# Queries kept times 1/128, maxima taken negated, and pooled scores of the last two half batches made one group at a time

## The chip, the cores and the metric

The kernel runs on 1 core of one Trainium2 chip. The metric is device time in microseconds (us), lower is better. One program computes everything in one launch: TensorE (PE) multiplies, VectorE (DVE), ScalarE (ACT) and GpSimd (POOL) work on the results, SyncE (SP) issues the DMAs.

## The reference

Two stages follow each other, all in float32. The first is attention on q, k, v of 2 batches, 8 heads, 576 positions and 64 columns, in two forms that are added:

```python
q_d = q.reshape(B, H, S // 4, 4, D).mean(axis=3)      # the same for k and v: 144 pooled positions
out_d = softmax(scale * q_d @ k_d.T) @ v_d             # scale = 1/8
out_up = np.repeat(out_d, 4, axis=2)
mask = np.abs(pos[:, None] - pos[None, :]) < 4         # each position sees 7 neighbours
out_local = softmax(where(mask, scale * q @ k.T, -1e9)) @ v
attn_out = out_up + out_local
```

The second takes the 1152 x 512 result as tokens x and adds four experts: `out += p[:, e:e+1] * (relu(x @ w1[e]) @ w2[e])`, with w1 of 512 x 1024, w2 of 1024 x 512 and p the normalised domain probabilities.

## The kernel before

The program is a list of named steps. Each step has an engine, names that it depends on, and a function that issues its instructions (`step`, line 163). `ORDER` (lines 22 to 95) is a table of all step names written out by hand: the steps are issued in that order, and each engine works off its own instructions in the order in which they were issued. `ENGINE` (line 20) moves single steps to another engine.

Attention runs in four half batches, a0 to a3 (two batches, two halves of 288 queries each). Steps of half batch a2 are named `a2.something`. For each half batch:

- `qt` transposes the queries with PE into PSUM, and `qte` copies them out into the tile qT (4 pairs of heads; three by ACT, one by DVE, line 171 or 173). In a0 the sums of four queries are made by `qds`, `qdt` and `qde`; in the others by `qd`, DVE reductions of qT (line 338), into the tile qd.
- Local attention goes in three blocks t of 96 queries: `sc` scores (line 497), `madd` adds a mask, `max`, `sub`, `exp`, `sum`, `eps`, `rec`, `norm`, `blk` transposes, `pv` times the values, `xs` adds the pooled part. In a0 the mask enters PSUM by a matmul (line 487).
- Pooled attention goes in four groups g of two heads: `ds` scores (`dscores`, line 640), `dm` maxima (line 664), `dn` the maxima times -SCD (line 672, SCD = 1/128), `de` exponentials on ACT with the negated maximum as bias and SCD as scale (line 677), `da` and `db` (lines 687, 689) turn sums into factors, `dq` multiplies by them (line 694, on POOL or DVE), `dt` transposes, `dc` copies, `dv` multiplies by pooled values, `xd` copies out.

Pooled scores, transposed queries and keys, transposed probabilities and products share three buffers of PSUM (the pool `ps_g`). `PAIRS` (lines 633 to 635) says which groups are issued together: in `dscores` the first `ds` of a pair takes buffers for both groups and issues their matmuls in turn, and the second `ds` issues nothing. Groups 0 and 2 read rows 0 to 63 of PE, groups 1 and 3 rows 64 to 127 (p0, line 649).

```python
PAIRS = {(x, y): ((0, 1), (2, 3)) for x in ("a0", "a1", "a2", "a3") for y in "sv"}
PAIRS["a3", "s"] = ((0, 1), (2,), (3,))
```

Expert 0 (`m00` to `m03`, four pieces of tokens) is woven into the attention as soon as tokens are there: `m` and `o` are its matmuls (lines 759 and 784), `r` and `l` split the hidden values (766, 770), `g` writes into the sum (791). Its weights are split by `whi` (ACT) and `wlo` (POOL, line 288, four instructions in a row per step). `warm` steps are matmuls without use (line 214). Experts 1 to 3 come behind, from about 184 us on, as one stretch of matmuls.

Of the kernel before, what the change touches and what calls it, by code (L numbers as in the profile page):

```python
# [10 lines left out]
AF = mybir.ActivationFunctionType  # L11
ALU = mybir.AluOpType
AX = mybir.AxisListType
# [16 lines left out]
    a0.dn1 k01te.0 a0.exp0 warm39 a0.sc2.0 warm7 k01t.3 warm1 a0.exp1 a0.dm0 a0.de1 a0.dn0 a0.sum1 a0.de0 a0.da1  # L30
    k01te.2 a0.da0 a0.db0 a0.sum0 a0.db1 a0.ds2 a0.ds3 a0.dm2 a0.dn2 a0.dm3 k01te.3 warm9 a0.sc2.1 warm35 warm38
    a0.dq0 a0.dt0 a0.dc0 a0.eps0 a0.dq1 a0.dn3 a0.rec0 a0.max2 a0.de2 a0.sub2 warm28 warm27 a0.dt1 a0.norm0 a0.da2
    a0.dc1 a0.db2 a0.dq2 a0.de3 a0.da3 a0.eps1 a0.db3 a0.blk0.1 a0.rec1 a0.exp2 a0.blk0.0 a0.sum2 a0.dq3 a0.norm1
    whi100.1 wlo100.1 a0.eps2 a0.blk1.1 a0.rec2 a0.blk1.0 warm26 a0.dv1 a0.dv0 a0.dt2 a0.dc2 a0.norm2 whi101.0
    a0.dt3 a0.dv2 warm8 a0.dc3 warm44 a0.pv0 a0.dv3 a1.qt.1 whi100.0 a0.xd a0.xs0 a1.qt.3 warm45 a0.pv1 a1.qt.2
    a0.blk2.0 a0.blk2.1 vw02 k10r.3 raw200 k10r.2 praw raw201 k10r.1 a0.xh0 a0.xs1 a0.xl0 wlo100.0 a1.start a1.qte.1
    a1.qte.3 wlo101.0 a1.qte.2 a0.pv2 a0.xs2 a0.xh2 a1.qt.0 whi200.1 whi101.1 wlo101.1 whi200.0 a1.qte.0 a0.xh1
    a0.xl2 a1.qd.1 a0.xl1 a1.qd.0 a1.sc1.1 a1.sc2.1 a1.sc2.0 warm32 a1.sc0.1 m00.m0 a1.ds0 a1.ds1 m00.m3 a1.dm0
    a1.dn0 a1.de0 a1.madd2 a1.dm1 a1.da0 wlo200.1 a1.dn1 a1.sc0.0 a1.ds2 wlo200.0 m00.r0 m00.l0 a1.madd0 whi201.1
    a1.de1 whi201.0 m00.r3 a1.db0 a1.dq0 a1.da1 a1.max2 a1.dm2 m00.m2 a1.sc1.0 a1.dt0 a1.db1 a1.dn2 a1.madd1 a1.dc0  # L40
    a1.de2 a1.da2 a1.ds3 kstart1 a1.dq1 m00.m1 m00.r2 m00.r1 a1.max0 m00.l3 a1.dm3 a1.dn3 a1.db2 wlo201.1 m00.l1
    a1.sub0 a1.dq2 a1.sub2 a1.dt1 m00.m6 a1.de3 a1.dc1 m00.m4 m00.r4 a1.exp0 a1.exp2 k11r.3 vw03 k11r.0 k10r.0
    k11r.1 k11r.2 vw04 vw05 v11n.1 v10n.1 a1.da3 a1.dv1 a1.dv0 a1.db3 a1.max1 a1.dq3 m00.l2 a1.dt2 k10t.2 m00.o00
    a1.dt3 a1.dc2 a1.dc3 m00.r6 k10te.2 a1.sum2 a1.sum0 m00.l4 wlo201.0 a1.eps0 a1.sub1 m00.m5 a1.dv3 k10t.0 a1.dv2
    k10t.1 m00.o01 m00.m7 a1.eps2 gate a1.rec2 a1.rec0 a1.norm0 m00.l6 a1.blk0.0 a1.norm2 a1.exp1 k10te.0 m00.r5
    m00.l5 a1.sum1 a1.eps1 k10te.1 a1.xd a1.blk0.1 k11t.1 a1.pv0 k11te.1 a1.rec1 a1.norm1 m00.r7 a1.xs0 a1.blk2.1
    m00.l7 a1.blk2.0 a1.blk1.1 k10t.3 k11t.0 m00.o10 m00.o02 k11t.3 k11t.2 k11te.0 k10te.3 a1.blk1.0 a1.pv2 k11te.3
    k11te.2 k11d.1 a1.pv1 a1.xs1 a1.xh1 a1.xl1 a1.xs2 a1.xh2 a1.xh0 a2.start a1.xl0 a1.xl2 k10d.0 k10d.1 m00.o11
    m00.o03 m00.g0 a2q.3 a2q.2 a2q.1 a2q.0 m00.o12 a2.qt.2 a2.qt.0 a2.qt.1 m01.m0 a2.qte.1 a2.qte.0 m01.r0 a2.qd.0
    k11d.0 m01.m1 v11d.1 a2.qte.2 a2.qt.3 a2.qte.3 a2.qd.1 a2.ds0 m00.o13 a2.sc0.1 a2.sc0.0 m00.g1 m01.l0 a2.ds1  # L50
    m01.m3 a2.dm1 a2.dn1 v11n.0 v10n.0 a2.de1 a2.madd0 a2.dm0 a2.dn0 a2.de0 a2.da0 a2.da1 a2.max0 a2.db0 m01.r3
    m01.r1 a2.dq0 v10d.1 v10d.0 a2.ds2 m01.m2 m01.r2 a2.db1 m01.l1 a2.dq1 m01.l2 a2.dm2 a2.dn2 a2.sc2.1 a2.sc2.0
    a2.sc1.0 a2.dt0 a2.sc1.1 a2.ds3 a2.dc0 a2.dt1 a2.madd1 a2.de2 a2.da2 a2.max1 m01.l3 a2.madd2 a2.sub1 vw12 a3q.2
    v11d.0 vw10 a3q.1 a3q.3 vw11 a3q.0 m01.m6 m01.m4 m01.r4 a2.dc1 a2.max2 a2.db2 a2.exp1 m01.l4 a2.dm3 a2.dn3
    a2.sub2 a2.exp2 a2.de3 m01.m5 m01.r5 m01.o10 a3.qt.1 a2.sum1 a2.dq2 a2.da3 m01.l5 m01.r6 a2.db3 a3.start a2.dv0
    a2.dv1 a2.dt2 m01.o00 m01.m7 a2.dq3 a2.dc2 a2.dt3 m01.o11 m01.l6 a2.sub0 a2.exp0 a2.dc3 a2.sum0 a2.eps1 a2.rec1
    a2.norm1 a2.eps0 a3.qte.1 a2.rec0 a2.norm0 a2.blk1.0 m01.o12 a2.dv2 a3.qt.0 a3.qt.2 m01.o01 a2.dv3 m01.r7
    a2.sum2 a2.blk0.0 a2.eps2 a2.rec2 a2.blk1.1 a2.norm2 a3.qte.2 a2.xd a3.qte.0 a2.blk0.1 a2.pv0 a2.blk2.1
# [3 lines left out]
    a3.exp1 a3.de1 m02.r1 a3.dn2 m01.g1 a3.da1 a3.db1 a3.dq1 m02.l1 a3.dn0 m02.r0 a3.madd0 m02.l0 a3.dt1 a3.de2
    a3.de0 m02.r4 a3.sum1 m02.m3 m02.m6 a3.max0 a3.da0 a3.madd2 a2.xh2 a3.db0 a3.eps1 m02.r6 m02.l4 a3.da2 a3.db2
    a3.sub0 a3.dq2 m02.m7 a3.dt2 a3.ds3 m02.l6 a2.xl2 a3.rec1 a3.exp0 m02.r3 m02.l3 a3.dm3 m02.m2 m02.r2 a3.dc2
    a3.dc1 a3.dn3 m02.l2 m02.o10 m02.o00 m02.r7 a3.sum0 a3.max2 a3.de3 a3.dq0 a3.eps0 a3.rec0 a3.da3 a3.norm1
    a3.sub2 a3.exp2 a3.norm0 a3.blk0.0 a3.db3 a3.dq3 m02.o01 m02.o02 a3.dv2 a3.dv1 a3.dt0 a3.dc0 a3.blk0.1 a3.pv0
    a3.dt3 a3.dc3 m02.l7 a3.sum2 a3.blk1.1 a3.eps2 a3.rec2 a3.dv0 a3.blk1.0 a3.norm2 a3.blk2.1 a3.blk2.0 m02.o03
    a3.dv3 a3.pv1 a3.pv2 m02.o11 a3.xd a3.xs1 a3.xs0 a3.xh0 a3.xs2 a3.xh1 a3.xl1 a3.xh2 m02.o12 a3.xl0 m02.o13
    a3.xl2 endattn m03.m3 m02.g1 wl10 m02.g0 x1.s0 m03.m4 m03.r3 x1.s1 m03.m0 m03.l3 m03.r4 x1.s2 m03.l4 x1.h m03.m1
    ws10 m03.r0 xn.l m03.l0 m03.m7 x1.l m03.r1 wh10 m03.l1 m03.m2 x2.s0 m03.r7 xn.h x3.s0 m03.m5 m03.r2 m03.l7  # L70
    m03.l2 wo10 m03.m6 m03.r5 m03.l5 wl11 m03.o00 x2.s1 m03.r6 m03.o20 m03.l6 x2.h x3.s1 m03.o01 x2.l m03.o10 x3.s2
# [1028 lines left out]
```

## Time and profile before

| what | value |
|---|---|
| time before, median of 3 runs (lowest to highest) | 475.59 us (473.67 to 476.49) |
| the profiled execution: its own time, its span | 472.98 us, 471.2 us |
| mean granted clock of PE | 0.982 |
| PE busy | 455.3 us, 97% of the span |
| DVE, ACT, POOL busy | 274.2, 162.6, 58.8 us |

Busy time is counted from the start of an instruction to its end; consecutive instructions of one engine overlap by some hundredths of a microsecond, so the length of a step is better read from the starts of two rows than from the length of one. A row of the timeline merges equal instructions (x8), and in brackets stands how long the engine was idle before it and which instruction ended that. One float32 matmul of the program is two pieces in the rows.

### The profile page before, as it was taken

What the parts mean: (1) busy time and instruction counts of PE and PEld (TensorE: products, weight loads), DVE (VectorE), ACT (ScalarE), POOL (GpSimd) and SP (SyncE); (2) the same over time, 40 slices, a digit from 0 to 9 for tenths busy, and PEclk for the clock granted to TensorE, in tenths of its full rate; (3) what the DMA queues carried; (4) which work ended last, traced back from release to release, by engine and by line L of the source; (5) the groups of instructions that cost most, each with busy time, mean ns of one, the idle gap of its engine ahead of it and who ended that gap; (6) DMA issues with size and microseconds to landing.
All of it is one profiled execution on the core that took longest, in us unless ns stands there. A gap on an engine that the chain in (4) does not pass through costs nothing.

```text
span 471.2 us, 8887 instructions
## 1 busy us (share of the span) xinstructions
PE 455.3 (97%) x3786; PEld 406.1 (86%) x3786; DVE 274.2 (58%) x481; ACT 162.6 (35%) x277; POOL 58.8 (12%) x89
## 2 busy tenths in 40 slices
...
GB/s 177 223 234 191 71 56 124 97 3 46 24 0 47 2 45 135 45 46 90 118 17 0 1 89 1 45 91 113 22 1 0 90 1 46 46 0 45 57 56 46
DMA packets 49575, 29.92 MB, mean 63 GB/s; under 512 B 26816, under 2 KB 43392, under 8 KB 49536
## 3 DMA queue, kind: packets, MB, share of 16 engines
...
q14 instruction: 9, 0.07, 0.1%
...
## 4 chain that ended last, share of the span: by engine, by line
PE 84%; DVE 6%; POOL 3%; DMA 2%; ACT 1%; SPq 1%; issue 1%; ACTq 0%; POOLq 0%
PE X L965 16%; PE Z L965 8%; PE Y L965 4%; PE m03h L759 4%; PE m03o L784 3%; POOL wlo L288 3%; PE m02h L759 3%; PE m02o L784 2%; PE m01o L784 2%; PE m00o L784 2%; PE m00h L759 2%; PE o L1022 1%; PE o28None L1022 1%; PE o18None L1022 1%; PE o36None L1022 1%
## 5 line engine op out<-in xcount | busy, mean ns | idle before, releaser
L1004 ACT ACTIVATE hh<-H 128x1024 fp32r<-128x1024 f32 (+1 forms) x30 | 28.9, 973 | 92.1 <-PE o30None L1022 4.9
L1007 DVE SCALAR_TENSOR_TENSOR ho<-H,hh 128x1024 fp32r<-128x1024 f32 (+1 forms) x30 | 33.5, 1117 | 24.3 <-ACT hh L1004 24.3
L917 DVE TENSOR_TENSOR wo<-r,wh 128x1792 fp32r<-128x1792 f32 x12 | 24.3, 2022 | 23.0 <-PE Z L965 18.9
L974 ACT ACTIVATE H<-X 128x576 f32<-128x576 f32 x24 | 15.6, 649 | 55.6 <-PE X L965 55.6
L965 PE MATMUL X<-xc,wh 128*128 128x288 f32 x192 | 33.2, 295 | 0.0
L965 PEld LDWEIGHTS X<-xc,wh 128*128 128x128 f32 x192 | 28.2, 188 | 0.0
L288 POOL TENSOR_TENSOR wlo<-raw,whi 128x256 fp32r<-128x256 f32 x28 | 21.2, 790 | 2.7 <-ACT whi L171 2.6
L965 PE MATMUL X<-xhi,wo 128*128 128x288 f32 x96 | 20.7, 296 | 0.0
L965 PE MATMUL X<-xlo,wh 128*128 128x288 f32 x96 | 20.6, 296 | 0.0
L965 PE MATMUL X<-xhi,wh 128*128 128x288 f32 x96 | 20.6, 295 | 0.0
L965 PE MATMUL X<-xc,wo 128*128 128x288 f32 x96 | 20.5, 295 | 0.0
L171 ACT CAST wh<-r 128x1792 fp32r<-128x1792 f32 x12 | 20.2, 1687 | 0.3 <-DVE r L909 0.3
L171 ACT CAST v<-q 128x1024 fp32r<-128x1024 f32 x12 | 12.2, 1044 | 15.7 <-PE o18None L1022 7.2
L978 DVE TENSOR_TENSOR H<-H,Z 128x576 f32<-128x576 f32 x12 | 9.0, 748 | 13.9 <-PE Z L965 13.9
L965 PE MATMUL Z<-xc,wh 128*128 128x288 f32 x96 | 16.6, 294 | 0.0
L965 PEld LDWEIGHTS X<-xhi,wo 128*128 128x128 f32 x96 | 15.6, 188 | 0.2
L965 PEld LDWEIGHTS X<-xlo,wh 128*128 128x128 f32 x96 | 15.4, 188 | 0.0
L965 PEld LDWEIGHTS X<-xhi,wh 128*128 128x128 f32 x96 | 15.4, 188 | 0.0
L965 PEld LDWEIGHTS X<-xc,wo 128*128 128x128 f32 x96 | 15.4, 188 | 0.0
L940 DVE TENSOR_TENSOR v<-q,v 128x1024 fp32r<-128x1024 f32 x12 | 14.6, 1220 | 0.9 <-ACT v L171 0.9
L978 DVE TENSOR_TENSOR H<-H,Y 128x576 f32<-128x576 f32 x12 | 9.0, 748 | 10.4 <-PE Y L965 6.3
L784 PE MATMUL m03o<-whi,m03t 128*128 128x512 f32 x48 | 15.0, 390 | 0.0
(457 smaller groups left out, 1186.1 us busy)
## 6 DMA issues: line engine op xcount, KB each, us to landing
...
```

What stands on the lines that cost most here:

```text
L171: nc.scalar.copy(out_, in_)
L288: eng.tensor_tensor(a[:, us], b[:, us], c[:, us], ALU.subtract)
L759: nc.tensor.matmul(ps[:, :n], w[:, d, cc:cc + P], x[:, d, n0:n0 + n], start=i == 0, stop=i == len(terms) - 1,)
L784: nc.tensor.matmul(ps[:, cs], T[f"{nm}t{f}"][:, hpart, cc:cc + P], w[:, f % 4, cs], start=f == 0 and x == 0, stop=f == KF - 1 and x == 2,)
L917: engine(f"wo{e}{i}").tensor_tensor(w, T[f"r{e}{i}"], f32(T[f"wh{e}{i}"]), ALU.subtract)
L940: engine(f"vo{e}{q}").tensor_tensor(w[:, 1], T[f"q{e}{q}"], f32(w[:, 0]), ALU.subtract)
L965: nc.tensor.matmul(ps[:, n, :NH // 2], w[:, d * P:(d + 1) * P], x[:, d, n * (NH // 2):(n + 1) * (NH // 2)], start=u == 0 and first_, stop= ...
L974: nc.scalar.mul(dst, at("Z" if c == "t22" else "X"), -1.0)
L978: nc.vector.tensor_tensor(dst, dst, at({"h11": "Y", "h12": "Z", "h22": "X"}[c]), ALU.add)
L1004: nc.scalar.activation(htile("hh", t, u), hrows(t, u), AF.Relu)
L1007: nc.vector.scalar_tensor_tensor(htile("ho", t, u), hrows(t, u), 0.0, f32(htile("hh", t, u)), ALU.max, ALU.subtract)
L1022: nc.tensor.matmul(T[o][:, cs], T[f"{hpart}{e}{t}"][:, f % 4 * 2 + f // 4], T[f"v{e}{q}"][:, w, f % 2 * 512 + cs.start:f % 2 * 512 + cs.stop],
```

## The change

The tile qT (and in a0 the tile qd) holds queries times SCD = 1/128, a power of two. Pooled scores then come out of PE already scaled: `dn` is dropped (16 instructions), `dm` takes the maximum with its sign turned, and `de` takes no scale. The local scores are smaller by 128 too, so their exponential has the scale 16 in place of 1/8, and the two mask constants are multiplied by 1/128. The 16 evictions `qte` (13 on ACT, 3 on DVE) and the one `qde` (DVE) multiply where they copied. In `PAIRS` the pooled scores of a2 and a3 are now issued one group at a time. In `ORDER` the names `dn` are gone and `a2.dt1` stands ahead of `a2.dc0`; all else is as before.

```diff
+    assert SCD == 2.0 ** -7
...
+    def scaled(name, out_, in_, by):
+        if steps[name][0] == "A":
+            nc.scalar.mul(out_, in_, by)
+        else:
+            engine(name).tensor_scalar(out_, in_, by, None, ALU.mult)
...
-        nc.vector.memset(mask[0:32, 0, 0:R], NEG)
-        nc.vector.memset(mask[96:128, 3, KW - R:KW], NEG)
+        nc.vector.memset(mask[0:32, 0, 0:R], NEG * SCD)
+        nc.vector.memset(mask[96:128, 3, KW - R:KW], NEG * SCD)
...
-        transposed(f"{a}.qt", src, srcdeps, lambda hp: T[f"{a}qT"][:, hp, 0:HT], [f"{a}.start"])
+        transposed(f"{a}.qt", src, srcdeps, lambda hp: T[f"{a}qT"][:, hp, 0:HT], [f"{a}.start"], SCD)
         if a == "a0":
-            pooled_rows(f"{a}.qd", "q0n", start_qd, [])
+            pooled_rows(f"{a}.qd", "q0n", start_qd, [], SCD)
...
-            nc.scalar.activation(wide(t), wide(t), AF.Exp, scale=SC)
+            nc.scalar.activation(wide(t), wide(t), AF.Exp, scale=SC / SCD)
...
-        PAIRS["a3", "s"] = ((0, 1), (2,), (3,))
+        PAIRS["a2", "s"] = PAIRS["a3", "s"] = ((0,), (1,), (2,), (3,))
...
-                axis=AX.X, op=ALU.max,
-            )
-
-        def dneg(g):
-            i0 = heads(g)[0]
-            mxs = dmx()[:, i0:i0 + 3:2]
-            nc.vector.tensor_scalar(mxs, mxs, -SCD, None, ALU.mult)
+                axis=AX.X, op=ALU.max, negate=True,
+            )
...
-                    bias=dmx()[:, h:h + 1], scale=SCD, accum_out=T[f"{a}dsm"][:, h:h + 1],
+                    bias=dmx()[:, h:h + 1], accum_out=T[f"{a}dsm"][:, h:h + 1],
...
-            step(n("dn"), "V", [n("dm")], lambda g=g: dneg(g))
-            step(n("de"), "A", [n("dn")], lambda g=g: dexps(g))
+            step(n("de"), "A", [n("dm")], lambda g=g: dexps(g))
```

What this does to the order on two engines is shown at three places. The first is DVE in a0, from the maxima of groups 1 and 0 (a0sd are the pooled scores, a0dmx the maxima, a0dsm the sums of `de`, kT the transposed keys). Before:

```order
L664 TENSOR_REDUCE a0dmx<-a0sd_412 72x2
L672 TENSOR_SCALAR a0dmx<-a0dmx 72x2
L664 TENSOR_REDUCE a0dmx<-a0sd_411 72x2
L672 TENSOR_SCALAR a0dmx<-a0dmx 72x2
L553 TENSOR_REDUCE a0sm_457<-a0pm_408 128x8
L687 TENSOR_SCALAR a0dsm<-a0dsm 72x2
L173 COPY kT_120<-k01t_417 128x4x72
```

And now:

```order
L676 TENSOR_REDUCE a0dmx<-a0sd_412 72x2
L676 TENSOR_REDUCE a0dmx<-a0sd_411 72x2
L565 TENSOR_REDUCE a0sm_455<-a0pm_408 128x8
L694 TENSOR_SCALAR a0dsm<-a0dsm 72x2
L179 COPY kT_120<-k01t_417 128x4x72
```

The two small multiplications are gone; the first TENSOR_SCALAR that reads and writes SBUF is now the one behind `de`. The other 14 go in the same way.

The second place is PE in a2, at the first pooled scores (m00o is a product of expert 0, a2sl are local scores). Before:

```order
L650 MATMUL a2sd_1325<-kd_912,a2qd 72x144
L650 MATMUL a2sd_1326<-kd_912,a2qd 72x144
L650 MATMUL a2sd_1325<-kd_912,a2qd 72x144
L650 MATMUL a2sd_1326<-kd_912,a2qd 72x144
L784 MATMUL m00o_1181<-whi_853,m00t_1054 128x512
```

And now:

```order
L662 MATMUL a2sd_1317<-kd_905,a2qd 72x144 x2
L790 MATMUL m00o_1173<-whi_847,m00t_1046 128x512
L790 MATMUL m00o_1173<-wlo_931,m00t_1046 128x512
L790 MATMUL m00o_1173<-whi_847,m00t_1046 128x512
L790 MATMUL m00o_1173<-whi_847,m00t_1152 128x512
L790 MATMUL m00o_1173<-wlo_931,m00t_1152 128x512
L790 MATMUL m00o_1173<-whi_847,m00t_1152 128x512
L509 MATMUL a2sl<-kT_904,a2qT 32x32 x32
L662 MATMUL a2sd_1361<-kd_905,a2qd 72x144 x2
```

Group 1, which was in turn with group 0, now stands behind a product of expert 0 and the local scores. In a3 the first two groups are parted in the same way, by twelve such products and the local scores.

The third place is PE in a2, at the last two groups (a2pdt are transposed probabilities). Before:

```order
L650 MATMUL a2sd_1415<-kd_912,a2qd 72x144
L650 MATMUL a2sd_1416<-kd_912,a2qd 72x144
L650 MATMUL a2sd_1415<-kd_912,a2qd 72x144
L650 MATMUL a2sd_1416<-kd_912,a2qd 72x144
L759 MATMUL m01h_1421<-xhi,wlo_550 128x256 x4
L759 MATMUL m01h_1421<-xhi,whi_548 128x256 x4
L759 MATMUL m01h_1421<-xlo,whi_548 128x256 x4
L497 MATMUL a2sl<-kT_911,a2qT 32x32 x48
L702 MATMUL a2pdt_1490<-ident,a2pd_1398 72x72 x4
L497 MATMUL a2sl<-kT_911,a2qT 32x32 x16
L702 MATMUL a2pdt_1513<-ident,a2pd_1391 72x72 x4
```

And now:

```order
L662 MATMUL a2sd_1405<-kd_905,a2qd 72x144 x2
L765 MATMUL m01h_1408<-xhi,wlo_546 128x256 x4
L765 MATMUL m01h_1408<-xhi,whi_544 128x256 x4
L765 MATMUL m01h_1408<-xlo,whi_544 128x256 x4
L509 MATMUL a2sl<-kT_904,a2qT 32x32 x48
L709 MATMUL a2pdt_1476<-ident,a2pd_1388 72x72 x4
L509 MATMUL a2sl<-kT_904,a2qT 32x32 x16
L662 MATMUL a2sd_1497<-kd_905,a2qd 72x144 x2
L709 MATMUL a2pdt_1500<-ident,a2pd_1382 72x72 x4
```

Group 3 moved to just ahead of the second transposes `a2.dt1`.

## Rows read from the trace of the kernel before

**Rows 1.** Busy time by engine in four stretches; at the end granted clock, DMA share, GB/s.

```profile
22.37:25.78 3.41, 1.63 (x76) 1.18 (x76) 3.22 (x11) 2.13 (x9) 2.39 (x4) 1.00 1.03 227
25.78:39.43 13.65, 13.51 (x154) 11.55 (x139) 10.84 (x35) 7.79 (x19) 10.71 (x18) 0.50 0.86 242
56.50:59.91 3.41, 3.41 (x19) 3.19 (x19) 1.70 (x5) 0.58 (x4) 3.27 (x6) 0.50 0.07 17
...
120.00:140.00 20.00, 20.00 (x294) 18.42 (x294) 15.35 (x50) 6.92 (x28) 1.38 (x2) 1.00 0.01 2
```

**Rows 2.** Groups of DVE's line L672 (`dn`): busy us, mean ns of one, idle before.

```profile
L672 DVE TENSOR_SCALAR a0dmx<-a0dmx 72x2 f32<-72x2 f32 x4 | 2.1, 531 | 0.1
...
L672 DVE TENSOR_SCALAR a1dmx<-a1dmx 72x2 f32<-72x2 f32 x4 | 1.3, 327 | 0.1
```

**Rows 3.** Timeline of a0, 21.3 to 25.6 us: start, length, engine, what, idle before.

```profile
21.86 1.26 POOL L428 TENSOR_TENSOR v01n<-v01n 72x512 f32<-72x512 f32 x1
22.06 1.09 DVE L672 TENSOR_SCALAR a0dmx<-a0dmx 72x2 f32<-72x2 f32 x1
...
23.86 0.54 POOL L251 MEMSET vw<- 4x512 f32 x1
...
24.13 0.47 PE L321 MATMUL k01t<-ident,kr 72*128 72x72 f32 x4 [1.41 <-ACT a0pd L677]
...
25.35 0.66 POOL L694 TENSOR_TENSOR a0pd<-a0pd,a0dsm 72x288 f32<-72x288 f32 x1 [0.94 <-DVE a0dsm L689]
```

**Rows 4.** Timeline of POOL and of DVE in a1, 51 to 55 us.

```profile
51.18 0.67 POOL L694 TENSOR_TENSOR a1pd<-a1pd,a1dsm 72x288 f32<-72x288 f32 x1 [0.21 <-DVE a1dmx L672]
51.80 2.78 POOL L288 TENSOR_TENSOR wlo<-raw,whi 128x256 fp32r<-128x256 f32 x4
...
52.32 2.29 DVE L687 TENSOR_SCALAR a1dsm<-a1dsm 72x2 f32<-72x2 f32 x1 [0.46 <-ACT a1pd L677]
```

**Rows 5.** Timeline of PE in a3: one group of pooled scores alone.

```profile
123.75 0.71 PE L650 MATMUL a3sd<-kd,a3qd 64*72 64x144 f32 x4
124.39 1.02 PE L497 MATMUL a3sl<-kT,a3qT 64*32 64x32 f32 x96
```

**Rows 6.** Timeline of PE in a2, 84 to 95 us.

```profile
84.36 0.46 PE L650 MATMUL a2sd<-kd,a2qd 64*72 64x144 f32 x2
85.66 0.71 PE L650 MATMUL a2sd<-kd,a2qd 64*72 64x144 f32 x6 [0.83 <-DVE a2qT L173]
86.30 0.50 PE L784 MATMUL m00o<-whi,m00t 128*128 128x512 f32 x1
...
88.80 0.74 PE L759 MATMUL m01h<-xhi,wlo 128*128 128x256 f32 x4 [0.16 <-DVE acc L791]
...
90.41 0.90 PE L650 MATMUL a2sd<-kd,a2qd 64*72 64x144 f32 x8
91.24 0.74 PE L759 MATMUL m01h<-xhi,wlo 128*128 128x256 f32 x4
...
94.80 0.44 PE L702 MATMUL a2pdt<-ident,a2pd 72*72 72x72 f32 x4 [0.26 <-DVE a2pts L173]
```

**Rows 7.** Timeline of PE in a3, 115 to 117 us.

```profile
115.29 0.46 PE L650 MATMUL a3sd<-kd,a3qd 64*72 64x144 f32 x2
116.45 0.71 PE L650 MATMUL a3sd<-kd,a3qd 64*72 64x144 f32 x6 [0.70 <-DVE a2x L590]
117.09 0.50 PE L784 MATMUL m01o<-whi,m01t 128*128 128x512 f32 x1
```

**Rows 8.** Groups of instructions by line: busy us, mean ns of one, idle before.

```profile
L974 ACT ACTIVATE H<-X 128x576 f32<-128x576 f32 x24 | 15.6, 649 | 55.6 <-PE X L965 55.6
L976 ACT COPY H<-X 128x576 f32<-128x576 f32 x12 | 7.7, 640 | 15.2 <-PE X L965 15.2
...
L173 DVE COPY a2qT<-a_qt 128x288 f32<-128x288 f32 x1 | 0.7, 653 | 0.0
...
L791 DVE TENSOR_SCALAR acc<-m00o,pr 128x512 f32<-128x512 f32 x2 | 1.5, 746 | 1.5 <-PE m00o L784 1.5
```

More of the change, by code (lines that the diff above doesn't have):

```diff
@@ L29 @@
     k00de k01r.0 a0.max0 a0.sub0 k01t.1 warm11 k01t.0 a0.max1 k01te.1 a0.sub1 a0.ds1 warm3 a0.ds0 k01t.2 a0.dm1
[L30 to L58, printed above, removed]
+    k01te.0 a0.exp0 warm39 a0.sc2.0 warm7 k01t.3 warm1 a0.exp1 a0.dm0 a0.de1 a0.sum1 a0.de0 a0.da1 k01te.2 a0.da0
@@ new lines @@
+    a0.db0 a0.sum0 a0.db1 a0.ds2 a0.ds3 a0.dm2 a0.dm3 k01te.3 warm9 a0.sc2.1 warm35 warm38 a0.dq0 a0.dt0 a0.dc0
+    a0.eps0 a0.dq1 a0.rec0 a0.max2 a0.de2 a0.sub2 warm28 warm27 a0.dt1 a0.norm0 a0.da2 a0.dc1 a0.db2 a0.dq2 a0.de3
+    a0.da3 a0.eps1 a0.db3 a0.blk0.1 a0.rec1 a0.exp2 a0.blk0.0 a0.sum2 a0.dq3 a0.norm1 whi100.1 wlo100.1 a0.eps2
+    a0.blk1.1 a0.rec2 a0.blk1.0 warm26 a0.dv1 a0.dv0 a0.dt2 a0.dc2 a0.norm2 whi101.0 a0.dt3 a0.dv2 warm8 a0.dc3
+    warm44 a0.pv0 a0.dv3 a1.qt.1 whi100.0 a0.xd a0.xs0 a1.qt.3 warm45 a0.pv1 a1.qt.2 a0.blk2.0 a0.blk2.1 vw02 k10r.3
@@ new lines @@
+    raw200 k10r.2 praw raw201 k10r.1 a0.xh0 a0.xs1 a0.xl0 wlo100.0 a1.start a1.qte.1 a1.qte.3 wlo101.0 a1.qte.2
+    a0.pv2 a0.xs2 a0.xh2 a1.qt.0 whi200.1 whi101.1 wlo101.1 whi200.0 a1.qte.0 a0.xh1 a0.xl2 a1.qd.1 a0.xl1 a1.qd.0
+    a1.sc1.1 a1.sc2.1 a1.sc2.0 warm32 a1.sc0.1 m00.m0 a1.ds0 a1.ds1 m00.m3 a1.dm0 a1.de0 a1.madd2 a1.dm1 a1.da0
+    wlo200.1 a1.sc0.0 a1.ds2 wlo200.0 m00.r0 m00.l0 a1.madd0 whi201.1 a1.de1 whi201.0 m00.r3 a1.db0 a1.dq0 a1.da1
+    a1.max2 a1.dm2 m00.m2 a1.sc1.0 a1.dt0 a1.db1 a1.madd1 a1.dc0 a1.de2 a1.da2 a1.ds3 kstart1 a1.dq1 m00.m1 m00.r2
@@ new lines @@
+    m00.r1 a1.max0 m00.l3 a1.dm3 a1.db2 wlo201.1 m00.l1 a1.sub0 a1.dq2 a1.sub2 a1.dt1 m00.m6 a1.de3 a1.dc1 m00.m4
+    m00.r4 a1.exp0 a1.exp2 k11r.3 vw03 k11r.0 k10r.0 k11r.1 k11r.2 vw04 vw05 v11n.1 v10n.1 a1.da3 a1.dv1 a1.dv0
+    a1.db3 a1.max1 a1.dq3 m00.l2 a1.dt2 k10t.2 m00.o00 a1.dt3 a1.dc2 a1.dc3 m00.r6 k10te.2 a1.sum2 a1.sum0 m00.l4
+    wlo201.0 a1.eps0 a1.sub1 m00.m5 a1.dv3 k10t.0 a1.dv2 k10t.1 m00.o01 m00.m7 a1.eps2 gate a1.rec2 a1.rec0 a1.norm0
+    m00.l6 a1.blk0.0 a1.norm2 a1.exp1 k10te.0 m00.r5 m00.l5 a1.sum1 a1.eps1 k10te.1 a1.xd a1.blk0.1 k11t.1 a1.pv0
@@ new lines @@
+    k11te.1 a1.rec1 a1.norm1 m00.r7 a1.xs0 a1.blk2.1 m00.l7 a1.blk2.0 a1.blk1.1 k10t.3 k11t.0 m00.o10 m00.o02 k11t.3
+    k11t.2 k11te.0 k10te.3 a1.blk1.0 a1.pv2 k11te.3 k11te.2 k11d.1 a1.pv1 a1.xs1 a1.xh1 a1.xl1 a1.xs2 a1.xh2 a1.xh0
+    a2.start a1.xl0 a1.xl2 k10d.0 k10d.1 m00.o11 m00.o03 m00.g0 a2q.3 a2q.2 a2q.1 a2q.0 m00.o12 a2.qt.2 a2.qt.0
+    a2.qt.1 m01.m0 a2.qte.1 a2.qte.0 m01.r0 a2.qd.0 k11d.0 m01.m1 v11d.1 a2.qte.2 a2.qt.3 a2.qte.3 a2.qd.1 a2.ds0
+    m00.o13 a2.sc0.1 a2.sc0.0 m00.g1 m01.l0 a2.ds1 m01.m3 a2.dm1 v11n.0 v10n.0 a2.de1 a2.madd0 a2.dm0 a2.de0 a2.da0
@@ new lines @@
+    a2.da1 a2.max0 a2.db0 m01.r3 m01.r1 a2.dq0 v10d.1 v10d.0 a2.ds2 m01.m2 m01.r2 a2.db1 m01.l1 a2.dq1 m01.l2 a2.dm2
+    a2.sc2.1 a2.sc2.0 a2.sc1.0 a2.dt0 a2.sc1.1 a2.ds3 a2.dt1 a2.dc0 a2.madd1 a2.de2 a2.da2 a2.max1 m01.l3 a2.madd2
+    a2.sub1 vw12 a3q.2 v11d.0 vw10 a3q.1 a3q.3 vw11 a3q.0 m01.m6 m01.m4 m01.r4 a2.dc1 a2.max2 a2.db2 a2.exp1 m01.l4
+    a2.dm3 a2.sub2 a2.exp2 a2.de3 m01.m5 m01.r5 m01.o10 a3.qt.1 a2.sum1 a2.dq2 a2.da3 m01.l5 m01.r6 a2.db3 a3.start
+    a2.dv0 a2.dv1 a2.dt2 m01.o00 m01.m7 a2.dq3 a2.dc2 a2.dt3 m01.o11 m01.l6 a2.sub0 a2.exp0 a2.dc3 a2.sum0 a2.eps1
@@ L59 @@
+    a2.rec1 a2.norm1 a2.eps0 a3.qte.1 a2.rec0 a2.norm0 a2.blk1.0 m01.o12 a2.dv2 a3.qt.0 a3.qt.2 m01.o01 a2.dv3
+    m01.r7 a2.sum2 a2.blk0.0 a2.eps2 a2.rec2 a2.blk1.1 a2.norm2 a3.qte.2 a2.xd a3.qte.0 a2.blk0.1 a2.pv0 a2.blk2.1
     a2.blk2.0 a2.pv1 a3.qt.3 m01.o02 vw14 vw13 vw15 a2.pv2 a3.qte.3 a3.sc1.0 m01.l7 a3.qd.0 a2.xs1 a2.xh1 a2.xs0
     a2.xh0 a3.qd.1 a2.xl0 a2.xl1 a3.ds0 m01.o13 m01.o03 a3.sc1.1 a3.sc0.1 m01.g0 a3.madd1 a3.ds1 m02.m1 m02.m5
-    a3.ds2 m02.r5 a3.dm1 a2.xs2 a3.dm0 a3.sc2.0 a3.sc0.0 a3.sc2.1 m02.m0 m02.m4 m02.l5 a3.dm2 a3.dn1 a3.max1 a3.sub1
@@ L62 @@
[L62 to L71, printed above, removed]
```

75 lines of the change are left out of this document (46 added, 29 removed).

## The prediction

> **What bounds the kernel now.** I first read busy time by engine over the stretches of the program. From about 56 us on PE is the bound: between 120 and 140 us it is busy 20.00 of 20.00 us [rows 1], and behind attention it never waits again. Whatever the change does there counts only as PE time added or PE waiting taken away. Before that, from 20 to 55 us, no engine is full for long. PE is busy 1.63 of 3.41 us ahead of 25.78, then runs at half its clock (0.50, the 1.2 GHz level) until 39.43, busy 13.51 of 13.65 us, with DVE at 10.84 in the same time [rows 1]. In this part a chain through DVE, ACT and POOL sets the pace, and what shortens it moves all that follows.
>
> Then I read the line that the change removes. In a0 the four `dn` take 531 ns each on average, in a1 327 ns [rows 2], for two numbers per partition; they are that long where POOL is at work. The timeline shows the longest: `dn1` starts 0.20 us into a POOL instruction of 1.26 us and ends at 23.15, just behind that one's end at 23.12 [rows 3]. Last I read the timeline of PE around the pooled scores of a2 and a3, where the pairs are split [rows 5 to 7].
>
> **The change, part by part.** The sum is against the profiled execution, 472.98 us with its span of 471.2; the median of the runs, 475.59, lies 2.61 above it, and I carry that difference along.
>
> *Evictions that multiply.* 13 `qte` on ACT become a scaled ACTIVATE, 3 `qte` and the `qde` on DVE a TENSOR_SCALAR. On ACT the same shape takes 649 ns as scaled ACTIVATE and 640 as COPY [rows 8]: 9 ns each, 0.1 us in all over four half batches if every one lay on the path, and only one or two of a half batch do. On DVE no row has the new form with this shape. The nearest are 653 ns for the COPY of 288 columns and 746 for a TENSOR_SCALAR out of PSUM on 512 [rows 8]; by the second an eviction costs no more than now, so I take nothing, with 0.1 us for the four at the far end (93 ns for one that lies on the path). The scale of the exponentials and the mask constants change numbers only.
>
> *Maxima with the sign turned.* No row has `dm` with a turned sign. I take its time as unchanged; 16 of them would have to grow by 60 ns each to make 1 us, so 0 to 0.3 us is my bound, and a gain has no source.
>
> *`dn` in a0.* Behind `dn1` stand `de1` and `de0` on ACT, then `da0`, `db0`, then `dq0` on POOL at 25.35, 2.20 us after `dn1`'s end at 23.15; PE idles 1.41 us in front of a key transpose that needs a buffer `de1` has read [rows 3]. Without `dn1`, `de1` can start where `dn1` started, 22.06, and 2.20 us on makes 24.26. POOL is then still in a memset until 23.86 + 0.54 = 24.40 [rows 3]. So `dq0` comes 25.35 - 24.40 = 0.95 earlier; I take 0.9 for the handover. The other three `dn` of a0 hide: `de2` and `de3` also wait for buffers that PE must have read. PE starts its stretch of 13.5 busy microseconds 0.9 earlier and has little slack in it [rows 1]. Bounds: 0 (the wait turns up elsewhere, below) and 2.1, all four [rows 2]. I take **-0.9**.
>
> *`dn` in a1.* Here POOL leads: `dq1` starts at 51.18 after 0.21 us of waiting for DVE, then four pieces of `wlo` run for 2.78, and the `da` of group 2 sits on DVE from 52.32 for 2.29 us, until they are done [rows 4]. Earlier `dn` and `db` save POOL the wait of 0.21 and a little ahead of it: **-0.3**, with 0 and 1.3, all four [rows 2], as bounds.
>
> *The first pair of a2 split.* Now PE issues the first piece of work of group 0 at 84.36, then waits 0.83 us, because group 1's buffer still holds transposed queries that DVE copies out late; the pair ends at 86.30 [rows 6], 1.94 in all. One group alone takes 124.39 - 123.75 = 0.64 [rows 5], as four pieces; a pair of eight takes 91.24 - 90.41 = 0.83 [rows 6]. So splitting adds PE work: the halves of a pair, on different rows of the array, run beside each other, single groups don't. Apart they cost 2 x 0.64 = 1.28, but group 1 now stands behind a product and the local scores, and its buffer is free by then. That saves 1.94 - 1.28 = 0.66, and the 0.16 that `m01` waited for a gather on DVE [rows 6] is covered by group 1's 0.64: -0.82. DVE's `dm1` waits for the later group 1, with `madd0` and `dm0` queued behind it; but PE reaches the end of group 1 at 84.36 + 0.64 + (88.80 - 0.16 - 86.30) + 0.64 = 87.98, and DVE comes from the gather no earlier than that product's end 1.3 us sooner than now, so nothing is late.
>
> *The second pair of a2.* 0.83 becomes 2 x 0.64: +0.45. The second group stands ahead of `dt1`, which waits 0.26 now for a copy [rows 6]; that wait is covered: +0.19 in the sum. Both pairs together **-0.63**.
>
> *The first pair of a3.* From 115.29 to 117.09 it takes 1.80, 0.70 of it waiting for group 1's buffer until DVE has read a product of a2 [rows 7]. Split: 1.28. **-0.52**. The other two groups of a3 are single already.
>
> The sum is -0.9 - 0.3 - 0.63 - 0.52 = -2.35, so 470.63 for such an execution and 475.59 - 2.35 = **473.2** at the median. That is almost exactly 0.5% below (2.38 us, 473.21), which is about what a measurement of this kernel can tell from no change.
>
> **The rivals.**
>
> *The clock stays up in a0.* Ahead of the fall at 25.78 PE was busy 1.63 of 3.41 us [rows 1]; about 1 us of its idle time goes, the 1.41 in front of the key transpose above all [rows 3]. If the clock stays at 2.4 GHz, PE's 13.51 us at half clock shrink and DVE, busy 10.84 of 13.65, is next: up to 13.65 - 10.84 = 2.8 more. Half of that makes 475.59 - 2.35 - 1.4 = 471.8. Against it: no row says how much of the idle time has to go, and other waits stay. Likewise the fall at 56.50, 3.41 us with PE full [rows 1], could go (up to 1.7) or stay.
>
> *The wait moves on.* It was not `dn` that was slow but DVE's way into SBUF beside POOL. The next TENSOR_SCALAR behind it, `da`, is of the same form and can stand into the next POOL instruction. Then the a0 and a1 terms go and -1.15 is left: 474.4. For it: `da` already stood 2.29 us in a1 [rows 4].
>
> *One more long stand.* With other timing another `da` meets a run of `wlo` as that one did: up to +2.29, which leaves -0.06: 475.5. What decides is whether DVE gets in between two pieces. The Trainium skill, in "SBUF — State Buffer", section "Who interferes with whom", says that of a VectorE instruction in a two-port mode and a GpSimd one the later blocks until the other instruction has ended. `dn1` agrees, 23.15 against 23.12 [rows 3]; the `da` of a1 differs, since 2.29 us is over three pieces of 2.78 / 4 = 0.70 [rows 4], and the measurement decides. By the rule alone this rival would cost at most 0.7 and end at 473.9.
>
> *The split only costs* (the one on the other side). Where PE is the bound, three split pairs add 0.45 to 0.64 each, up to 3 x 0.64 = 1.92, and what ends the waits of 0.83 and 0.70 could be not the buffer but the pooled queries, which DVE reduces in the same moments. It decides at 84.36 and 115.29: if group 0's second half also waits there, nothing is saved. Then -1.2 + 1.92 = +0.7: 476.3. Against it: group 0's first pieces started before the wait [rows 6, 7].
>
> **How the numbers follow.** The forecast has 0.42, the clock 0.18, the moved wait 0.17, the long stand 0.13, the split that only costs 0.10. Faster by over 0.5%: half of the forecast (it lies on the bound), nearly all of the clock's case and a little of the others, 0.21 + 0.17 + 0.04 = 0.42. Slower by over 0.5% (above 477.97): a part of the last two, 0.07. Within: 0.51. The range takes in the clock's case to half beyond its middle, 470.2, and above the split that only costs with some 0.7 for the spread of the runs, 477.0.
>
> **What would show it.** After the change `dq0` of a0 starts about 0.9 us earlier; the wait of 1.41 us shrinks to about 0.4; no wait stands inside the first pooled scores of a2 and a3; each of the eight single groups takes 0.64; `m03` begins about 2.3 us earlier. I am wrong if the clock's stretches change, if a `da` stands longer in POOL's way, or if scaled evictions take visibly longer than the copies.

## The result and the profile after

| | before | after |
|---|---|---|
| time beside each other, median (lowest to highest) | 475.31 us (473.19 to 476.62) | 471.22 us (468.09 to 471.79) |
| ratio | | 0.991, interval 0.989 to 0.994 |
| the profiled execution: its own time, its span | 472.98, 471.2 us | 471.22, 469.4 us |
| mean granted clock of PE | 0.982 | 0.971 |
| PE busy | 455.3 us, 97% | 458.7 us, 98% |
| DVE, ACT, POOL busy | 274.2, 162.6, 58.8 us | 270.3, 162.6, 59.0 us |

The change is faster by 4.1 us, or 0.9%. The forecast was 473.2, so 2.4 us faster, on the edge of what can be told from no change; the time lies in its range, with three quarters more gain than was counted.

Executions of one kernel are not alike here. They differ in when PE's clock falls from 2.4 to 1.2 GHz, and with it in time, by 5 us and more. This page happens to have the long fall. The first view is busy time over stretches of the kernel after (length, PE, PEld, DVE, ACT, POOL busy, granted clock, DMA share, GB/s); the first row is all of its time at 1.2 GHz until the program's end:

```profile
15.10:42.41 27.31, 27.00 (x383) 22.56 (x384) 17.79 (x54) 15.71 (x39) 21.12 (x29) 0.50 0.84 226
56.74:59.73 2.99, 2.99 (x24) 2.86 (x24) 2.37 (x8) 1.12 (x5) 2.83 (x5) 1.00 0.00 0
```

Before had 13.65 us at that level from 25.78 on and 3.41 more from 56.50 on [rows 1]. In after the clock fell earlier and stayed low for longer, and PE comes to the first transposes of probabilities in a0 2.1 us later (28.13 beside 26.07); but its second row, from where PE takes up m00h again, has full clock, where before [rows 1] was at half. Compared directly, these two traces mix the change with the clock. The first experiment gives a better partner.

The split pairs answer to [rows 6] and [rows 7]; PE in a2 and a3 after:

```profile
84.32 0.71 PE L662 MATMUL a2sd<-kd,a2qd 64*72 64x144 f32 x4
84.95 0.50 PE L790 MATMUL m00o<-whi,m00t 128*128 128x512 f32 x1
...
86.54 0.76 PE L509 MATMUL a2sl<-kT,a2qT 64*32 64x32 f32 x64
87.22 0.71 PE L662 MATMUL a2sd<-kd,a2qd 64*72 64x144 f32 x4
87.86 0.74 PE L765 MATMUL m01h<-xhi,wlo 128*128 128x256 f32 x4
...
93.33 0.71 PE L662 MATMUL a2sd<-kd,a2qd 64*72 64x144 f32 x4
93.97 0.44 PE L709 MATMUL a2pdt<-ident,a2pd 72*72 72x72 f32 x4
...
114.08 0.71 PE L662 MATMUL a3sd<-kd,a3qd 64*72 64x144 f32 x4
114.72 0.50 PE L790 MATMUL m01o<-whi,m01t 128*128 128x512 f32 x1
...
118.35 0.71 PE L662 MATMUL a3sd<-kd,a3qd 64*72 64x144 f32 x4
118.99 0.74 PE L765 MATMUL m02h<-xhi,wlo 128*128 128x256 f32 x4
```

Neither first group waits any more, and a single group takes 0.63 to 0.64 us from start to the next start. In a1 the third `da` and what follows it answer to [rows 4]:

```profile
53.90 2.80 POOL L294 TENSOR_TENSOR wlo<-raw,whi 128x256 fp32r<-128x256 f32 x4
54.66 1.37 DVE L694 TENSOR_SCALAR a1dsm<-a1dsm 72x2 f32<-72x2 f32 x1 [0.45 <-ACT a1pd L684]
56.74 0.73 PE L765 MATMUL m00h<-xhi,wlo 128*128 128x256 f32 x4 [1.31 <-DVE m00t L776]
```

The groups by form of before and of after (count, then shortest, median and longest ns) show what the scaled evictions and the negated maxima cost. Before:

```profile
L171 ACT COPY a2qT<-a_qt x3: 669/670/712, 81.4 to 84.5; 128x288 f32<-128x288 f32 x3
L173 DVE COPY a2qT<-a_qt x1: 653/653/653, 85.0 to 85.0; 128x288 f32<-128x288 f32 x1
L664 DVE TENSOR_REDUCE a2dmx<-a2sd x4: 444/444/444, 89.0 to 99.4; 72x2 f32<-72x288 f32 x4
```

After:

```profile
L171 ACT ACTIVATE a2qT<-a_qt x3: 686/698/740, 81.3 to 84.4; 128x288 f32<-128x288 f32 x3
L173 DVE TENSOR_SCALAR a2qT<-a_qt x1: 660/660/660, 84.9 to 84.9; 128x288 f32<-128x288 f32 x1
L676 DVE TENSOR_REDUCE a2dmx<-a2sd x4: 443/444/453, 88.0 to 98.1; 72x2 f32<-72x288 f32 x4
```

That is 7 to 28 ns more for an eviction in a2; in the other half batches the middle value moves by -5 to +10 ns. Turning the sign costs nothing.

### The profile page after: what moved, and what is told of

It reads as the page before. It is cut to its first block, busy times and chain, and to the rows that moved or that the text cites. A ratio compares the mean times of both kernels' runs of the same rounds, so it can differ in the third digit from the quotient of the medians.

```text
span 469.4 us, 8869 instructions
## 1 busy us (share of the span) xinstructions
PE 458.7 (98%) x3786; PEld 409.3 (87%) x3786; DVE 270.3 (58%) x465; ACT 162.6 (35%) x277; POOL 59.0 (13%) x89
## 4 chain that ended last, share of the span: by engine, by line
PE 89%; POOL 4%; DVE 3%; issue 1%; DMA 1%; ACT 1%; SPq 0%; POOLq 0%; ACTq 0%
PE X L971 16%; PE Z L971 8%; PE Y L971 4%; PE m03h L765 4%; PE m03o L790 3%; POOL wlo L294 3%; PE m02h L765 3%; PE m01h L765 3%; PE m01o L790 2%; PE m02o L790 2%; PE m00o L790 2%; PE m00h L765 1%; PE o L1028 1%; PE o28None L1028 1%; PE o18None L1028 1%
```

## The experiments

Each ratio is to runs of the kernel before on the same chip.

| run | ratio (interval) | mean of its runs, us |
|---|---|---|
| e1_before, unchanged | 1.000 (0.997 to 1.002) | 474.70 |
| e2_split, split alone | 0.998 (0.996 to 1.001) | 473.69 |
| e3_scale, no dn, pairs kept | 0.995 (0.992 to 0.998) | 472.66 |
| e4_dnback, all dn back | 0.997 (0.994 to 1.000) | 473.53 |
| e5_after, the change | 0.989 (0.986 to 0.992) | 470.84 |
| e6_dn_a0 | 0.989 (0.985 to 0.993) | 470.60 |
| e7_dn_a1 | 0.993 (0.990 to 0.997) | 472.84 |
| e8_late_wlo | 0.994 (0.990 to 0.997) | 472.43 |
| e9_no_stand | 0.991 (0.988 to 0.994) | 469.98 |
| e10_before_no_stand | 0.998 (0.994 to 1.001) | 473.36 |
| e11_dn_a2a3 | 0.992 (0.989 to 0.996) | 470.82 |
| e12_no_stand_blk | 0.989 (0.986 to 0.992) | 470.37 |

Means of different groups of runs compare only by way of the kernel before beside them: it had 474.78 beside e1 to e4, 475.79 beside e5 to e8, 474.73 beside e9 to e11 and 475.50 beside e12.

Much of the spread within one kernel goes with the clock, so the runs tell more when compared at one clock. One straight line of time on mean granted clock for all 244 runs with a clock on record, with a level of its own for each kernel, has a slope of 1.9 us for 0.01 of clock. It puts the kernels this many us below the kernel before:

| e2 | e3 | e4 | after, e5 | e6 | e7 | e8 | e9 | e10 | e11 | e12 |
|---|---|---|---|---|---|---|---|---|---|---|
| 1.9 | 2.4 | 2.0 | 4.0 | 4.2 | 2.1 | 3.1 | 3.1 | 1.1 | 3.7 | 4.0 |

Each holds to 0.4 (e6 and e9, of six runs, to 0.6). This is an estimate: it takes out what a change does to the clock itself, and treats the chips as alike; with a term for each group of runs the values move by some 0.3. Below it is called the line.

**The kernel before again.** No edit.

> The kernel before once more, unchanged, for its clocks: the changed kernel's runs have a mean granted clock of 0.970 to 0.975 at 470.6 to 471.8 us, and one has 0.985 at 468.1. Theory A (terms of the prediction, the clock plays no part): the kernel before shows the 0.982 of its profile in most runs, 473 to 476 us whatever the clock. Theory B (the clock falls at either of two places in both kernels, and the profile of before, 472.98 us, was taken in the rarer state): most runs show about 0.970 at 475 to 476, few 0.98 at 473. Ratio to before 1.000 either way.

Its executions took 471.5 us at a clock of 0.985 and 476.1 to 476.7 at 0.968, so the clock plays a part, and theory A's flat picture falls; both kinds are common, against B's "most at 0.970". Its profile has the same fall as the one of after, 27.31 us long, which makes them a clean pair:

```profile
15.79:43.10 27.31, 27.03 (x384) 22.59 (x384) 18.61 (x58) 15.70 (x39) 21.56 (x29) 0.50 0.90 230
```

In its timeline the stand and the wait are those of before:

```profile
55.38 2.29 DVE L687 TENSOR_SCALAR a1dsm<-a1dsm 72x2 f32<-72x2 f32 x1 [0.46 <-ACT a1pd L677]
58.38 0.74 PE L759 MATMUL m00h<-xhi,wlo 128*128 128x256 f32 x4 [2.23 <-DVE m00t L770]
```

Matched instruction by instruction on PE, after is ahead by 0.73 us at 13.5 us, before anything that the change touches could matter (I take this for the spread of the first loads), by the same 0.72 at 53.3, by 1.64 at PE's m00h, and by 3.34 behind a3. So in this pair a0 gave nothing, a1 0.92 and the splits 1.70.

**One part alone, and dn put back.** e2: the kernel before with the split; e3: the kernel after without it; e4: the kernel after with `dn`:

```diff
# e2, in before
-        PAIRS["a3", "s"] = ((0, 1), (2,), (3,))
+        PAIRS["a2", "s"] = PAIRS["a3", "s"] = ((0,), (1,), (2,), (3,))
# e3, in after: the opposite
# e4, in after
-                axis=AX.X, op=ALU.max, negate=True,
+                axis=AX.X, op=ALU.max,
...
+            nc.vector.tensor_scalar(mxs, mxs, -1.0, None, ALU.mult)
```

> Only the pooled scores of a2 and a3 issued one group at a time (and a2's second transposes ahead of the first copy); the small multiplications dn and the unscaled queries stay. Theory A (the prediction's terms): -0.63 and -0.52, together -1.15 us, 474.2 beside 475.3. Theory B (the trace of the changed kernel: everything runs 1.15 earlier behind the split places of a2 and 0.55 earlier behind that of a3): -1.7 us, 473.6. Theory C (the splits only shift waits, and the gain is dn's): 0.

> The scaled queries and the negated maxima without dn, with the pairs of a2 and of a3 as they were before. Theory A (the prediction's terms): -0.9 in a0 and -0.3 in a1, so -1.2 us, 474.1 beside 475.3. Theory B (the rest of the measured -4.1 once the splits have given 1.7, by way of the long stand of a da in a1, 2.29 us before and 1.37 after, and the clock's second fall at 56.50, which the changed kernel's trace doesn't have): -2.4 us, 472.9, with no stretch at 1.2 GHz behind 50 us. Theory C (all is dn's): -4.

> The changed kernel with the 16 small multiplications dn put back on DVE at their old places, times -1.0, and the maxima's sign not turned; the scaled evictions and the split pairs stay. If the time comes from dn's absence, this lies 1.2 us (theory A) or 2.4 us (theory B) above the changed kernel, 472.4 or 473.6, which is where the split alone lies; if the scaled evictions cost or save something by themselves, it lies apart from the split alone by that much (the prediction says 0.0 to 0.1). dn in a0 has a mean of about 531 ns and in a1 of 327 ns again.

By the means the split alone gave 1.1 us, no `dn` alone 2.1, and e4, with `dn` back, is 1.3 below before where the change was 5.0 below in e5. Their intervals are about 2 us wide and choose neither for `dn` (1.2 or 2.4) nor for the split (1.15 or 1.7). The line does: 2.4 for no `dn`, 1.9 for the split, both on theory B's side with theory A's value outside, and the two add up to 4.3 where the change has 4.0. For the split the trace of e2 lies between. Its stretches at half clock in attention are as long as before's (13.65 and 3.41 us). It is 0.9 us behind before at the first pooled scores of a2 (85.28, 84.36), partly from a wait for loads of q, and 0.6 ahead at m02h (120.18, 120.76), so the splits gave 1.5 there. e4 and e2 agree (473.53, 473.69), so the scaled evictions cost nothing that shows.

**dn in one half batch.** In after, `negate=a not in ("a0",)` with `dn` times -1.0 for that half batch alone; likewise a1, and a2 with a3. e5 is the kernel after.

> The changed kernel once more, as the measure for the three beside it and for a second profile: 470.6 to 471.8 us in executions whose mean granted clock is 0.970 to 0.975, 468.1 at 0.985; no stretch at 1.2 GHz between 45 and 65 us. About 471.2 at the median, some 3.5 below the kernel before.

> The changed kernel with dn (times -1.0) put back in a0 alone, four instructions. Theory A (the prediction: dn1 of a0 holds the whole chain up): +0.9 us over the changed kernel. Theory B (two executions with the same stretch at 1.2 GHz, 27.31 us from 15 us on, show the same shift ahead of a0's dn and behind it): 0.0 where the clock falls at 15 us, at most a few tenths over all executions.

> The changed kernel with dn put back in a1 alone, four instructions. Theory A (the prediction): +0.3 us over the changed kernel. Theory B (dn in a1 decides how long the third da stands beside four pieces of wlo, 2.29 to 2.47 us with dn and 1.37 without, and so how long PE waits for m00t): +0.9 us, and +1.3 more in those executions where the clock then falls at 56 us, so +0.9 to +2.2; the third da of a1 takes over 2 us and the wait of PE for m00t is 2.2.

> The changed kernel with dn put back in a2 and a3, eight instructions. Both theories: 0.0, since the split pairs alone show the whole shift of 1.7 us behind a3; over 0.5 us would mean that part of what is put down to the splits is dn's.

`dn` in a0 costs nothing that shows (470.60 beside 470.84; 0.2 less than the change on the line, where 0.9 would stand out); in a1 it costs 2.0 us (472.84, or 1.9 on the line). Both are as theory B said. In a2 and a3, where both theories said 0.0, e11 is 3.9 us faster than the runs of before beside it, and e5 was 5.0; on the line `dn` costs 0.3 there, with 0.0 inside the interval. In e7 the long stand and, in the row of stretches under it, the second fall of the clock are back:

```profile
53.04 2.79 POOL L295 TENSOR_TENSOR wlo<-raw,whi 128x256 fp32r<-128x256 f32 x4
53.56 2.29 DVE L700 TENSOR_SCALAR a1dsm<-a1dsm 72x2 f32<-72x2 f32 x1 [0.46 <-ACT a1pd L690]
56.56 0.74 PE L774 MATMUL m00h<-xhi,wlo 128*128 128x256 f32 x4 [2.23 <-DVE m00t L785]
```

```profile
57.18:60.59 3.41, 3.41 (x19) 3.41 (x18) 1.98 (x6) 1.11 (x5) 3.15 (x5) 0.50 0.07 17
```

Why a0 gives nothing is in two traces with the long fall, after and e6, from the maxima of group 1 to the first transposes on PE. After:

```profile
23.99 0.82 DVE L676 TENSOR_REDUCE a0dmx<-a0sd 72x2 f32<-72x288 f32 x2 [1.84 <-PE a0sd L662]
28.13 0.69 PE L709 MATMUL a0pdt<-ident,a0pd 72*72 72x72 f32 x4
```

e6, with `dn` in a0:

```profile
25.76 0.45 DVE L677 TENSOR_REDUCE a0dmx<-a0sd 72x2 f32<-72x288 f32 x1 [1.84 <-PE a0sd L663]
29.90 0.69 PE L715 MATMUL a0pdt<-ident,a0pd 72*72 72x72 f32 x4
```

4.14 us in both, and 4.14 or 4.15 in the other five profiles with the early fall, e1 among them: PE, at half clock and without a gap, sets it. What holds a0 up where the clock falls late is told below.

**The stand taken away.** e8 moves the four pieces of `wlo201.1` on POOL from ahead of `a1.sub0` to behind `a1.sub2`. e9 and e10 put `a1.dq3` on POOL and the pieces behind it (with the issues of v11n and v10n, whose buffer they read), in after and in before; e12 moves `a1.blk0.1` up in e9:

```diff
# e9 in after, e10 in before (ENGINE, ORDER)
-'a1.dq3': 'V'
+'a1.dq3': 'G'
-a1.db2 wlo201.1 m00.l1
+a1.db2 m00.l1
-vw05 v11n.1 v10n.1 a1.da3
+vw05 a1.da3
-a1.dq3 m00.l2
+a1.dq3 wlo201.1 v11n.1 v10n.1 m00.l2
# e12, in e9
-m00.l6 a1.blk0.0 a1.norm2
+m00.l6 a1.blk0.0 a1.blk0.1 a1.norm2
```

> The changed kernel with the four pieces of wlo201.1 on POOL moved behind a1.sub2, so that they no longer run while the third da of a1 comes. If that stand of 1.37 us is what PE's wait of 1.31 us for m00t hangs on, the da takes 0.2 to 0.5 and everything behind runs up to 1.0 us earlier: 470.2. If the stand moves on to the fourth da (0.53 now), which would then meet the same pieces, nothing is gained, 471.2, and if the last group's exponentials and factors come later by it, up to 1 us is lost.

> The changed kernel with a1.dq3 on POOL in place of DVE and the four pieces of wlo201.1 behind it (and with them the issues of the loads of v11n and v10n, which need the buffer that they read), so that POOL waits for the fourth da and db before the pieces begin and no da of a1 can stand beside them. If PE's wait of 1.31 us for m00t hangs on the stand of the third da (1.37 us), all four da of a1 take 0.2 to 0.7, that wait shrinks to under 0.5 and the time is about 0.9 us below the changed kernel: 469.6 where that takes 470.5. If a later instruction of DVE stands beside the pieces in its place, or the product of expert 0 then waits for wlo, nothing is gained or up to 1 us is lost.

> The kernel before, with dn, its pairs and unscaled queries, and the same move of a1.dq3 and wlo201.1. Theory A (what is gained in a1 is the time of the dn themselves): 0 to 0.3 us faster at most, since all dn stay. Theory B (dn cost time in a1 only by making the third da stand 2.29 us beside the four pieces): the da take 0.2 to 0.7, PE's wait of 2.2 us for m00t shrinks to under 0.7, no stretch at 1.2 GHz begins between 50 and 65 us, and the time is 1.5 to 2.5 us below the kernel before, about 473, where the kernel before takes 475.

> The version of e9_no_stand with a1.blk0.1 on DVE moved ahead of m00.l5 and a1.sum1, since there PE came 1.0 us earlier at 56 us and gave it back at a1.pv0, where it waited 1.4 us until that transpose was done (67.61). If that is where the gain went, PE's wait there falls to about 0.5 and the time is 0.5 to 1.0 us below the changed kernel's 470 to 471: a ratio to the kernel before of 0.988 or less. If the wait of 0.6 for the loads of q in a2 grows by as much, or m00.l5 coming 0.9 later holds PE up, it stays at the changed kernel's time, ratio 0.989 to 0.991.

e8 lost 1.6 us in the mean and 0.9 on the line: the third `da` took 0.17, but the fourth met the pieces and stood longer than any before, and PE waited for m00t at a later place:

```profile
52.08 0.17 DVE L694 TENSOR_SCALAR a1dsm<-a1dsm 72x2 f32<-72x2 f32 x1 [0.46 <-ACT a1pd L684]
54.24 3.29 DVE L694 TENSOR_SCALAR a1dsm<-a1dsm 72x2 f32<-72x2 f32 x1 [0.59 <-ACT a1pd L684]
54.70 2.80 POOL L294 TENSOR_TENSOR wlo<-raw,whi 128x256 fp32r<-128x256 f32 x4
58.80 0.50 PE L790 MATMUL m00o<-whi,m00t 128*128 128x512 f32 x1 [1.48 <-DVE m00t L776]
```

In e9 no `da` of a1 takes over 0.8 and PE's wait for m00t is 0.2, but the ratio isn't below the change's, and at a clock of 0.984 to 0.985 its three runs take 470.3 at the median and after's three 469.5. PE waits 1.4 us later on, at a product that it now reaches too early, and 0.6 for loads of q:

```profile
67.72 0.88 PE L589 MATMUL a1pv<-ptb,vw 128*64 128x96 f32 x16 [1.41 <-issue]
...
80.05 0.94 PE L327 MATMUL a_qt<-ident,acc 72*128 72x72 f32 x12 [0.59 <-DMA acc<-in_q_dram]
```

In e12 the first of these fell to 0.4 and the second stayed, and the time is that of the change again. So the 0.9 us by which the change shortened PE's wait for m00t was worth having, what was left of it gave nothing in these versions, and none is faster than the change. e10 takes the stand out of the kernel before and keeps every `dn`: 1.4 us faster than the 474.73 of the runs beside it, in the mean, with an interval that reaches 1.001, and 1.1 faster on the line. Theory A allowed 0.3; theory B's 1.5 was not reached, and its profile has the 1.41 us wait at `a1.pv0` too, and no fall behind 50 us. With e7 this shows that `dn` in a1 costs time mainly by way of the stand, and not by its own length.

## Why the prediction was right, and where it was not

**Right in direction and range, not by all of its reasons.** The sum was -2.35, measured -4.1. That it fell no further off is partly luck: 0.9 counted for a0 isn't there, and 1.7 of a1 and 0.5 of the splits weren't counted. m03 begins at 149.38, 1.8 us earlier than in the profile that the forecast went by (151.14) and 3.3 earlier than in e1 (152.71); it was to be 2.3. One of the prediction's signs of being wrong came, since the clock's stretches changed, but they do so from one execution of a kernel to the next. By terms:

*Evictions and turned maxima.* Forecast 0 (to 0.3); nothing that shows by the groups and by e4 beside e2. Right.

*a0, forecast -0.9, measured 0.0 (e6).* This step failed. It took `dn1`'s 1.09 us [rows 3] for what holds a0 up. In e1, the same kernel, `dn1` takes 0.23, and in e2 0.45. Among the 14 profiles of this case seven have the late fall of the clock (25 to 27 us). In two of them alone, the one of before that I read and e10's, the first `dq` of a0 starts 0.9 us behind POOL's memset, so that `dn1` can count. In the five others `dq0` starts as POOL ends that memset, with `dn` (e2, e4) or without (e7, e8, e9); in the seven with the early fall PE at half clock sets the pace. `dn1` in e1, then POOL in e2:

```profile
25.20 0.23 DVE L672 TENSOR_SCALAR a0dmx<-a0dmx 72x2 f32<-72x2 f32 x1
...
25.35 0.54 POOL L251 MEMSET vw<- 4x512 f32 x1
25.86 1.28 POOL L694 TENSOR_TENSOR a0pd<-a0pd,a0dsm 72x288 f32<-72x288 f32 x2
```

In e9 `de1` came 1.28 us earlier than in before and `dq0` 0.78 later, since POOL was late with v, and PE's wait only changed its place [rows 3]:

```profile
25.61 0.54 POOL L257 MEMSET vw<- 4x512 f32 x1
26.13 1.28 POOL L701 TENSOR_TENSOR a0pd<-a0pd,a0dsm 72x288 f32<-72x288 f32 x2
26.84 0.69 PE L709 MATMUL a0pdt<-ident,a0pd 72*72 72x72 f32 x4 [1.35 <-POOL a0pd L701]
```

The rival that the wait moves on (0.17) had the outcome for a0, but not its cause: what holds a0 up is POOL's own queue, or PE at half clock, and not `da`.

*a1, forecast -0.3, measured about -2.0 (e7).* This term was mis-sized. The bound of 1.3 was too small as well, for it held only the time of the four `dn`. What they cost is the place of another instruction. From the transposes `a1.dt0` to the third `da` is 1.4 us before and after (50.93 to 52.32, 53.28 to 54.66). `wlo` began 0.87 behind the transposes before, as `dq1` waited 0.21 for DVE [rows 4], and begins 0.62 behind them now (53.90). So the `da` meets the second piece and not the first: it stands 1.37 us and not 2.29 [rows 4], and PE waits 1.31 for m00t and not 2.23. Before, then after:

```profile
50.93 0.45 PE L702 MATMUL a1pdt<-ident,a1pd 72*72 72x72 f32 x4 [0.95 <-POOL a1pd L694]
55.32 0.74 PE L759 MATMUL m00h<-xhi,wlo 128*128 128x256 f32 x4 [2.23 <-DVE m00t L770]
...
53.28 0.44 PE L709 MATMUL a1pdt<-ident,a1pd 72*72 72x72 f32 x4 [1.50 <-POOL a1pd L701]
```

All ten profiles that have the pieces in this place agree. With `dn` in a1 (before, e1, e2, e4, e7) `dq1` waits 0.21 to 0.83 for DVE and the `da` stands 2.29 to 2.47; without (after, e3, e5, e6, e11) `dq1` doesn't wait and the `da` stands 1.36 or 1.37. The rival of one more long stand named the right pair of instructions and the wrong sign.

*The second fall of the clock.* The rival of the clock (0.18) said that the fall at 56.50 "could go (up to 1.7) or stay", without tying it to a1. Among the profiles it comes only where PE has waited over 2 us ahead of m00h, in before, e2, e4 and e7, and not always there: e1 has the same wait and no fall. All profiles without `dn` in a1 lack it. The mean granted clock tells something of the other runs: 13.65 us and 3.41 at half clock make the 0.982 of before's profile. Of 115 runs of the kernel before 25 have this value, of 69 runs of after, e3, e6, e9, e11 and e12 none, of 12 of e8 one. Where the first fall is of 27.31 us, the mean doesn't separate the kernels: with 3.41 more it would be 0.968 on the span of before, where 17 runs have it, and 0.967 on the shorter one of after, where three of the 69 have it. Runs of before at 0.968 have a median of 476.4, those at 0.971 one of 475.0: if the second fall is what they differ by, it costs 1.4 us where it comes. The other half of that rival, that the fall in a0 goes, did not come true: the mean clock of after's runs (0.975) is that of before's (0.974).

*The splits, forecast -0.63 and -0.52, measured -1.15 and -0.55.* The buffer's waits went as said: 1.94 became 0.63 and 1.80 became 0.64, and each parted group 1 took its 0.64 [rows 5]. In a2 the first pair gave 0.91 (forecast 0.82) and the second cost 0.12 (forecast 0.19). Of the other 0.36, 0.22 is a wait that I had left out, from the last `m01h` to `m01o`, 0.69 before and 0.47 after:

```profile
98.86 0.63 PE L759 MATMUL m01h<-xlo,whi 128*128 128x256 f32 x4
99.55 0.50 PE L784 MATMUL m01o<-whi,m01t 128*128 128x512 f32 x1
...
98.03 0.64 PE L765 MATMUL m01h<-xlo,whi 128*128 128x256 f32 x4
98.50 0.40 PE L790 MATMUL m01o<-whi,m01t 128*128 128x512 f32 x1
```

In e2's trace beside before's a2 gave 0.97 and a3 0.53, so a2's excess over the forecast is smaller there; for both together the line has 1.9.

In the pair of traces 0.92 + 1.70 = 2.6 us are accounted for, and with 1.4 for the second fall, where before has it, 4.0. Runs at one clock, 0.970 to 0.971, differ by 3.2 at the median (474.99, 15 runs, and 471.77, 8 runs); what makes up the last 0.6 there wasn't found.
